# Gated recurrence and low-rank mixer on one core: a new instruction order, 96-row block totals, ReLU inside an add

## The chip, the cores and the metric

The kernel runs on one core of a Trainium2 chip. The metric is the device time of one execution in microseconds. Three executions of the kernel before took 645.2, 645.34 and 646.04 us; the median is 645.34. The profile is one further execution, 645.33 us, of which 643.6 us lie between its first and its last instruction (the span). TensorE's granted clock was 0.999 of full speed in it.

## The reference

There are two stages. The first is a gated linear recurrence with a complex gate, for 4 batches, 8 heads, 768 steps and a head width of 48:

```python
mag = np.sqrt(a_re * a_re + a_im * a_im)
scale = np.minimum(mag, 0.999) / (mag + 1e-06)
a_re_n, a_im_n = (a_re * scale, a_im * scale)
for t in range(S):
    new_re = ar * S_re - ai * S_im        # ar, ai: the gate at step t, per row of the state
    new_im = ar * S_im + ai * S_re
    kv = np.einsum('bhd,bhe->bhde', k[:, :, t], v[:, :, t])
    S_re, S_im = (new_re + kv, new_im)
    y[:, :, t] = np.einsum('bhd,bhde->bhe', q[:, :, t], S_re)
```

Its output, laid out as x with 4 batches, 768 tokens and 384 channels, goes through a mixer. It mixes tokens by a product of rank 32 and channels by two dense layers of width 1536:

```python
xt = x.transpose(0, 2, 1)
h = xt @ U @ V                            # U 768x32, V 32x768
u = x + h.transpose(0, 2, 1)
ch = np.maximum(u @ w_ch1, 0.0) @ w_ch2   # 384x1536, 1536x384
return (u + ch).astype(np.float32)
```

## The kernel before, in words

**Tiling.** The 3072 tokens (4 batches of 768) are cut into 24 chunks of 128. Two neighbouring chunks form a group, so there are 12 groups; six chunks (three groups) make a batch. A gate's decay is kept as a logarithm of its magnitude and a phase. Within a chunk the recurrence is written as products of scaled q, k and v; the state G is carried from chunk to chunk.

**Stages of a group.** `load_a` fetches a_re and a_im. `magnitudes` makes the log magnitudes `GL` with squares, logarithms and exponentials on ScalarE and adds on VectorE. For groups 3 to 11 (`SPLIT`) it also splits them into two parts for faster sums (`GS`). `within` makes running sums on TensorE and exponentials of them (`es`, `ef`). `totals` and `of_blocks` make sums of `GL` over 32 kinds of blocks of tokens, by products with the constant matrix `total` (line 711): for each chunk, four pairs of heads, the two heads of a pair in the lower and the upper half of the array's columns. ScalarE takes the exponential (`E`), and four transfers on SP's queue (line 697) place it in `T`, by which q and k are later scaled. `turns` and `angles` make the phases; a phase's last row is carried to the next chunk by a transfer on GpSimd's queue (line 750, `gate<-F`). `waves` makes cosines and sines (`cs`).

**Stages of a chunk.** `load_qkv` fetches q, k and v. `prep` scales and rotates q and k (`QKC`), and transposes them (`tr`, line 823) to `QK`. `chain` makes the products of neighbouring tokens (`inner`, lines 870 and 873; `corners`, line 937), picks them by masks into `DG`, places them by transfers into `AT` (line 924), scales `QK` by `T`, advances the state (`dk`, line 962, to `GM` and `G`), and makes the chunk's output `y` (lines 993 and 1001), which ScalarE copies to `xo`.

**Mixer.** `mixer(m)` takes two chunks, so there are 12 mixers, three a batch. The first of a batch needs all six chunks' `xo`: `rank` (line 1036) is their product with U, in 12 matrix products that accumulate in one tile, in four strips of 32 columns; ScalarE copies it to `r`. Then come the product with V (`mixed`, line 1052), an add to `xo`, the transposition `uTp` (line 1065), and the copy `uT` (line 1067), for each of its two chunks. `up` is the first dense layer (line 1077) with ReLU on ScalarE. From mixer 7 on (`FEWER`) `up_fewer` makes that layer from 15 products instead of 18 (`few`, line 1135): the first product to a part of `h` is copied there by ScalarE, later ones are added by VectorE, and a pass of ScalarE over `h` makes the ReLU. `down` and `down_two` (lines 1223 and 1266) are the second layer; their results are added to `xo` and stored.

**Weights.** A piece of w1, w2 or of U and V arrives as fp64 words (`stage`) and is converted by `single`: two scalings, a shift, an add, and a merge of the sign. Pieces with a number below `EARLY` have the scalings on VectorE, the others on ScalarE; the other three operations are VectorE's. The six pieces of w1 come first, then U and V, then the six of w2.

**What sets the order.** No scheduler orders the instructions when the kernel is built. Each operation is entered in a plan under an engine, a kind and a rank, and the table `ORDER` gives it its place; `Plan.order` sorts all operations by that number, and each engine runs its own in that order. SP and GpSimd issue their transfers in order too: a transfer that waits for a buffer holds back all that follow on the same queue. The table `SPARE` says how many filler products (`spare`, line 1396, whose result is not used) TensorE runs before an operation. There are 130 of them, all ahead of the first `up`. The costs in the calls (`PE(0.51, ...)`) are not used when the kernel is built.

## Time and profile before

| what | value |
|---|---|
| median of 3 runs | 645.34 us (645.2 to 646.04) |
| the profiled execution | 645.33 us |
| its span | 643.6 us |
| TensorE busy | 623.3 us (97%), 10242 records |
| weight loads busy | 552.9 us (86%) |
| VectorE busy | 515.3 us (80%), 933 instructions |
| ScalarE busy | 411.6 us (64%), 785 instructions |
| GpSimd busy | 38.4 us (6%) |
| transfers | 163316 packets, 45.72 MB; 153808 packets under 512 B |

Times are in microseconds from the span's start. A matrix product in fp32 appears as two records of TensorE, each with a weight load (PEld); a transposition and an fp32r product appear as one. "PE" in a busy share covers the filler too. `L379`, `L382` and `L376` are helpers (multiply, add, activation), so groups with these lines are told apart by their tiles. "SPq" is SP's queue: the time that it spent on issuing a transfer.

### The profile page before, as it was taken

To read this page: it belongs to the slowest core of one execution; us is meant where nothing else is said; L and a number is where in the kernel's file an instruction comes from. 1 tells how busy PE (TensorE), PEld (TensorE's weight loads), DVE (VectorE), ACT (ScalarE), POOL (GpSimd) and SP (SyncE) were. 2 spreads that over 40 slices of the span, in tenths; PEclk is the share of its full clock that TensorE was granted. 3 is DMA by queue.
4 is the path that set the end of the run, shared out by engine and by line. 5 is a ranking of instruction groups with operands and counts; after the bars stand their busy time and mean duration, and the time that the engine had idled before them with its cause. 6 is when DMAs were issued, how large, how long until landed. Compare 5 with 4: busy or idle time off the path is not lost.

```text
span 643.6 us, 23208 instructions
## 1 busy us (share of the span) xinstructions
PE 623.3 (97%) x10242; PEld 552.9 (86%) x10242; DVE 515.3 (80%) x933; ACT 411.6 (64%) x785; POOL 38.4 (6%) x79
## 2 busy tenths in 40 slices
PE   8998988999999999999999999999999999999997
PEld 7777777776889889789988988888999998999997
DVE  7999999687999879658969877787999884664653
ACT  7899988696887786666686786678355333212130
POOL 5000000000000000020020010010100000000010
PEclk9999999999999999999999999999999999999999
DMA  8755473625142362241331433411204010000010
GB/s 224 196 117 123 98 191 69 172 101 111 31 82 57 80 123 43 49 108 20 58 79 31 86 72 65 98 28 35 46 22 76 20 26 3 1 1 7 20 44 31
DMA packets 163316, 45.72 MB, mean 71 GB/s; under 512 B 153808, under 2 KB 160016, under 8 KB 163216
## 3 DMA queue, kind: packets, MB, share of 16 engines
q1 hardware_dynamic: 161008, 39.90, 28.6%
q0 software_dynamic: 2208, 4.35, 2.0%
q8 instruction: 80, 1.31, 0.9%
q14 instruction: 20, 0.16, 0.1%
HBM read 33.59 MB, written 4.72 MB: 60 GB/s over the span
## 4 chain that ended last, share of the span: by engine, by line
PE 76%; DVE 8%; DMA 5%; ACT 5%; SPq 3%; issue 2%; POOL 0%; DVEq 0%; ACTq 0%; POOLq 0%
PE down L1266 22%; PE up L1077 15%; PE few L1135 11%; PE tr L823 5%; PE y L1001 3%; PE dk L962 3%; PE inner L873 2%; PE y L993 2%; PE inner L870 2%; ACT gate L376 2%; DVE QK L379 1%; DMA qk<-in_k_dram 1%; PE mixed L1052 1%; PE mixed L1036 1%; DMA gate<-F 1%
## 5 line engine op out<-in xcount | busy, mean ns | idle before, releaser
L1077 PE MATMUL up<-uT,w 128*128 128x256 f32 x504 | 115.5, 381 | 1.3 <-ACT h L376 1.3
L379 DVE TENSOR_TENSOR QK<-QK,T 112x512 f32<-112x512 f32 (+2 forms) x144 | 102.6, 730 | 7.7 <-PE corners L937 3.3
L1077 PEld LDWEIGHTS up<-uT,w 128*128 128x128 f32 x504 | 93.5, 190 | 13.6 <-ACT h L376 1.7
L376 ACT ACTIVATE gate<-gate 128x768 f32<-128x768 f32 (+1 forms) x89 | 70.8, 799 | 11.5 <-DVE GS L759 5.6
L835 ACT COPY QK<-tr 112x512 f32<-112x512 f32 x96 | 53.7, 585 | 34.8 <-PE tr L823 34.3
L1266 PE MATMUL down<-w,h 128*128 128x192 f32 x396 | 73.1, 331 | 0.0
L1266 PEld LDWEIGHTS down<-w,h 128*128 128x128 f32 x396 | 64.0, 190 | 3.0 <-issue 2.0
L1143 ACT COPY h<-few 128x512 f32<-128x512 f32 x30 | 17.3, 586 | 66.6 <-PE few L1135 66.5
L823 PE MATMUL tr<-ident,QKC 128*112 128x128 f32 x384 | 53.9, 276 | 4.9 <-DVE QKC L379 3.4
L379 DVE TENSOR_TENSOR QKC<-qk,cs 128x768 f32<-128x768 f32 x48 | 45.5, 953 | 8.2 <-ACT cs L376 3.8
L823 PEld LDWEIGHTS tr<-ident,QKC 128*112 128x112 f32 x384 | 42.5, 133 | 11.1 <-DVE QKC L379 4.1
L382 DVE TENSOR_TENSOR h<-few,h 128x512 f32<-128x512 f32 x45 | 30.6, 689 | 22.2 <-PE few L1135 12.3
L382 DVE TENSOR_TENSOR xo<-down,xo 128x192 f32<-128x192 f32 (+1 forms) x79 | 30.1, 385 | 19.0 <-PE down L1266 18.9
L1396 PE MATMUL spare<-ident 128*128 128x128 f32 x260 | 40.1, 298 | 2.1 <-POOL ident masks.py:199 1.4
L1396 PEld LDWEIGHTS spare<-ident 128*128 128x128 f32 x260 | 35.5, 206 | 5.7 <-POOL ident masks.py:199 1.4
L1266 PE MATMUL down<-stage 128*128 128x192 f32 x198 | 37.4, 329 | 0.0
L1135 PE MATMUL few<-gate,w 128*128 128x128 f32 x280 | 36.4, 278 | 0.0
L1210 POOL DMA_DIRECT2D out_dram<-xo x32 | 18.8, 604 | 275.4 <-DVE xo L382 164.0
L1135 PEld LDWEIGHTS few<-gate,w 128*128 128x128 f32 x280 | 33.6, 192 | 0.4
L942 ACT COPY AT<-corners 32x128 f32<-32x128 f32 x96 | 24.3, 255 | 13.9 <-PE corners L937 12.4
L376 ACT ACTIVATE h<-up 128x512 f32<-128x512 f32 x42 | 24.6, 591 | 13.1 <-PE up L1077 13.1
L1266 PEld LDWEIGHTS down<-stage 128*128 128x128 f32 x198 | 32.1, 190 | 0.6 <-issue 0.2
(153 smaller groups left out, 1240.9 us busy)
## 6 DMA issues: line engine op xcount, KB each, us to landing
stage<-in_moe_w_ch_dram SPq DMA_DIRECT2D x12, 768.0 KB, 5.0
gate<-in_a_im_dram SPq DMA_DIRECT2D x24, 192.0 KB, 3.5
gate<-in_a_re_dram SPq DMA_DIRECT2D x24, 192.0 KB, 3.4
qk<-in_k_dram SPq DMA_DIRECT2D x24, 192.0 KB, 3.0
qk<-in_q_dram SPq DMA_DIRECT2D x24, 192.0 KB, 3.4
VP<-in_v_dram SPq DMA_DIRECT2D x24, 192.0 KB, 3.9
AT<-DG SPq DMA_DIRECT2D x96, 32.0 KB, 2.5
T<-E SPq DMA_DIRECT2D x48, 48.0 KB, 2.3
```

The lines of the kernel that those rows point to most:

```text
L376: return nc.scalar.activation(out=o, in_=i, func=f, **kw)
L379: nc.vector.tensor_tensor(out=o, in0=a, in1=b, op=OP.mult)
L382: nc.vector.tensor_tensor(out=o, in0=a, in1=b, op=OP.add)
L823: nc.tensor.transpose(out=get(*ps)[0:DQ, j], in_=get(*qkc)[:, hh * HH + j].rearrange("p u d -> p (u d)")[:, 0:DQ], identity=ident)
L835: nc.scalar.copy(out=to, in_=a)
L942: ACT(0.36, RR, lambda r=r, u=u: nc.scalar.copy(out=get(*ATi).rearrange("p (a u) t -> p a u t", u=2)[r:r + BLK, :, u, BLK:2 * BLK], in_=ge ...
L962: nc.tensor.matmul(out=get(*dk[r])[x:end, h], lhsT=get(*ks)[at, h, x // DP, 0:end - x], rhs=get(*VPi)[at, h], start=True, stop=True, tile_ ...
L1001: nc.tensor.matmul(out=get(*y[u])[side(r, u), p], lhsT=k_of(h, r * HC, HC), rhs=get(*(mid_G if r else ("G", i - 1)))[:, h], start=False, s ...
L1077: nc.tensor.matmul(out=get(*ps)[:, e], lhsT=w1[:, f, (ff + e) * 128:(ff + e + 1) * 128], rhs=get(*uT)[:, f], start=(f == 0), stop=(f == KD ...
L1135: nc.tensor.matmul(out=get(*ps)[:, q], lhsT=w()[:, q * 128:(q + 1) * 128], rhs=v[0](), start=(n == 0 and q == 0), stop=True, skip_group_ch ...
L1266: nc.tensor.matmul(out=get(*to)[:, part], lhsT=x(j), rhs=y[:, j], start=(first and j == 0), stop=(j == KH - 1), skip_group_check=not first)
L1396: nc.tensor.matmul(out=spare[0], lhsT=ident, rhs=ident, start=True, stop=True)
```

## The change

- Both tables, `ORDER` and `SPARE`, are replaced, so that operations of all engines stand in other places. The author's search for the new order allowed at most 3072 pieces of transfers under way at a time. There are 139 filler products.
- Block totals of groups 3 to 11: a pair of heads is one product with 96 columns of weights, four products a chunk in place of eight. `E` then holds the two heads of a pair in rows 0 to 47 and 48 to 95, and the four transfers to `T` write pieces of 32 elements in place of 128.
- `EARLY` is 4, and U and V are converted third, after two pieces of w1. So pieces 0, 1 (w1), 2 (U, V) and 3 (w1) are scaled on VectorE.
- Batch 0's `rank` is entered as three operations of four products, so that each can stand in a place of its own. The other batches' is one operation as before.
- The copy `uT` of a mixer's second chunk is ScalarE's; the first stays on VectorE.
- In `up_fewer`, the last add to a part of `h` is a custom VectorE operation that adds and limits the result to 0 and above; the pass for ReLU on ScalarE is dropped.

```diff
-    EARLY, SPREAD = 3, (0,)
+    EARLY, SPREAD = 4, (0,)
...
             for f in range(KD):
+                if p == 2:
+                    single(p, ("w1", p), ("UV", 0), UV, [tokens(moe_U), tokens(moe_V.rearrange("r (s m) -> (r s) m", m=m))])
+                    p += 1
+                    for n in range(NP):
+                        SP(0.45, ("load", 7), lambda n=n: nc.sync.dma_start(out=V[n * R:(n + 1) * R].rearrange("r (s m) -> r s m", m=m),
+                                                                   in_=UV[:, NCH * R:]), reads=[("UV", 0)], writes=[("V", 0, n)])
                 single(p, ("w1", p), ("w1", f, h), w1[:, f, h:h + WP], [tokens(moe_w_ch1[f * 128:(f + 1) * 128, h:h + WP])])
...
-                        in_=get(*e)[w * 64:w * 64 + D, 0:hi - lo].rearrange("p c h b -> p c (h b)")), [e], [tt + ((u, w),)])
+                        in_=get(*e)[w * 64:w * 64 + D, 0:hi - lo].rearrange("p c h b -> p c (h b)")) if g not in SPLIT else
+                       nc.sync.dma_start(out=get(*tt)[u * DP:u * DP + D].rearrange("p c (h w b) -> p c h w b", w=2, b=NTOT)[:, :, :, w],
+                                         in_=get(*e)[w * D:(w + 1) * D]), [e], [tt + ((u, w),)])
...
-            PE(0.51, R1, sums, [l, ("total", 0), ("sums", g)], [ps], way=1, takes=[e], steps=4 * HH)
+            def at_once():
+                for p in range(HH):
+                    h = (i - lo) * DM + p * 2 * D
+                    nc.tensor.matmul(out=get(*ps)[0:2 * D, p], lhsT=get(*l)[:, h:h + 2 * D], rhs=total, start=True, stop=True)
+            if g in SPLIT:
+                PE(0.4, R1, at_once, [l, ("total", 0), ("sums", g)], [ps], takes=[e], steps=2 * HH)
+            else:
+                PE(0.51, R1, sums, [l, ("total", 0), ("sums", g)], [ps], way=1, takes=[e], steps=4 * HH)
...
-            PE(2.07, R0, rank, [("UV", 0)] + [("xo", b * NCH + c) for c in range(NCH)], [ps], steps=2 * NP * NCH // MC)
+            rounds = range(NCH // MC)
+            for ks in [[k] for k in rounds] if b == 0 else [rounds]:
+                PE(0.69 * len(ks), R0, lambda ks=ks: rank(ks), [("UV", 0)] + [("xo", b * NCH + c) for c in range(NCH) if c % len(rounds) in ks] +
+                   [sums_r + (("k", ks[0] - 1),)] * (ks[0] > 0), [sums_r + (("k", k),) for k in ks], steps=2 * NP * len(ks))
...
-            DVE(c_dve(DM), R0, lambda: nc.vector.tensor_copy(out=get(*uT)[:, :, cc * CH:(cc + 1) * CH], in_=get(*tr)), [tr],
-                [uT + (cc,)])
+            to = lambda: get(*uT)[:, :, cc * CH:(cc + 1) * CH]
+            if cc:
+                ACT(c_act(DM) - 0.045, R0, lambda: nc.scalar.copy(out=to(), in_=get(*tr)), [tr], [uT + (cc,)])
+            else:
+                DVE(c_dve(DM), R0, lambda: nc.vector.tensor_copy(out=to(), in_=get(*tr)), [tr], [uT + (cc,)])
...
-                    else:
+                    elif left[to] > 1:
                         DVE(c_dve(n3 * CH), RU, lambda i=i, k=k: add(at(i, k), get(*ps), at(i, k)), [ps], [o])
+                    else:
+                        DVE(c_dve(n3 * CH), RU, lambda i=i, k=k: nc.vector._custom_dve(
+                            dve_ops.TENSOR_ADD_SAT, out=at(i, k), in0=get(*ps), in1=at(i, k), s0=math.inf, s1=0.0), [ps, o],
+                            [h + (n3 * i,), h + (n3 * i + 2,)])
-                    if not left[to]:
-                        ACT(c_act(n3 * CH) - 0.045, RU, lambda i=i, k=k: act(at(i, k), at(i, k), AF.Relu), [o],
-                            [h + (n3 * i,), h + (n3 * i + 2,)])
```

## The prediction

> **What bounds the kernel now.** I read the page's busy shares first, then busy time by stretch, then the waits of TensorE, and last the order of time where the first mixer begins.

> ```profile
> span 643.6 us, 23208 instructions
> ...
> PE 623.3 (97%) x10242; PEld 552.9 (86%) x10242; DVE 515.3 (80%) x933; ACT 411.6 (64%) x785; POOL 38.4 (6%) x79
> ...
> L1396 PE MATMUL spare<-ident 128*128 128x128 f32 x260 | 40.1, 298 | 2.1 <-POOL ident masks.py:199 1.4 <-issue 0.7
> ```
> ```profile
> 20.00:113.00 93.00, 83.25 (x2079) 67.58 (x2079) 88.79 (x148) 86.86 (x165) 0.00 (x0) 1.00 0.56 131
> ...
> 120.30:640.00 519.70, 515.93 (x7986) 465.88 (x7984) 404.09 (x736) 304.10 (x583) 29.79 (x47) 1.00 0.24 53
> ```
> ```profile
> PE up L1077 <- ACT h L376: 1.3, 1, 1.3
> PE y L1001 <- DVE QK L379: 1.1, 1, 1.1
> PE y L993 <- DMA AT<-DG: 0.7, 1, 0.7
> PE y L1001 <- issue: 0.4, 1, 0.4
> ```

> The columns of the stretches are length, then busy time of PE, its weight loads, VectorE, ScalarE, GpSimd. All of the 40 us of filler (`spare`) lies before the first mixer's `up`, so from 20 to 113 us a busy TensorE means little: VectorE is the bound (88.8 of 93 us, 4.2 idle). From 120.3 us, the first `up`, to 640 TensorE is busy 515.9 of 519.7 us, and its waits there (third fence) sum to 3.5. So there are two prices: what delays or hastens the first `up`, and what lengthens TensorE's own work after it. A shorter operation elsewhere pays only through one of these.

> **The change part by part.** All sums stand on the profiled execution (645.33, span 643.6; the median of the runs is 645.34, so nothing is converted).

> *Block totals (L711).* Eighteen blocks, two chunks for each of groups 3 to 11, go from eight 64- or 48-column products in two halves of the array to four 96-column ones. Two of them come before the first `up` beside filler; 16 lie in the saturated part.

> ```profile
> 180.62 0.65 PE L711 MATMUL tot<-total,GL 128*64 128x32 f32 x16
> 181.20 0.46 PE L937 MATMUL corners<-QK 112*32 112x32 f32 x32
> ```
> ```profile
> 474.23 1.06 PE L1135 MATMUL few<-gate 128*128 128x128 f32 x8
> 475.12 1.06 PE L1135 MATMUL few<-gate,w 128*128 128x128 f32 x8
> ```

> An fp32 product is two records. A block holds TensorE from 180.62 to 181.20, 0.58 us. By the trace's start times 0.09 of this is the change of the array's shape (the last `few` before an `inner` is followed after 205 ns, another `few` after 112), leaving 0.49. The loads of the 64-column half start 58 ns apart, those of the 48-column half 45, with only 32 columns streamed in either: weight loading sets the pace, and the halves load side by side. The new block is eight records in one row. If a 96-column load took no longer than the old pairs (0.49/8 = 61 ns), it would cost the same 0.49; if it took as long as a 128-column `few` (0.89/8 = 111), 0.89. By columns it lies between, 61 + 32/64 x 50 = 86, so 0.69: I take that, since 45, 58 and 111 rise evenly with the columns. That is +0.20 x 16 = +3.2 us. The instruction orders have 170 shape changes after the first `up` before and 166 after, -0.4. Sum +2.8, ends -0.4 (61 ns) and +6.0 (111). Fewer instructions, more time.

> [...]

> *Rank in three steps, end of the startup.*

> ```profile
> 110.84 0.56 DVE L382 TENSOR_TENSOR GM<-GM,dk 112x384 f32<-112x384 f32 x1 [0.43 <-PE dk L962]
> 112.65 0.64 PE L1001 MATMUL y<-G,QK 112*64 112x48 f32 x16
> 114.00 0.31 ACT L1012 COPY xo<-y 64x192 f32<-64x192 f32 x1
> 114.31 2.14 PE L1036 MATMUL mixed<-xo,UV 128*32 128x384 f32 x24
> 116.52 0.48 ACT L1039 COPY r<-mixed 128x384 f32<-128x384 f32 x1 [0.40 <-PE mixed L1036]
> 117.05 0.92 PE L1052 MATMUL mixed<-r,V 64*128 64x192 f32 x8
> 118.00 1.02 DVE L382 TENSOR_TENSOR xo<-mixed,xo 128x384 f32<-128x384 f32 x2 [0.21 <-PE mixed L1052]
> 120.34 7.98 PE L1077 MATMUL up<-uT,w 128*128 128x256 f32 x36
> ```

> Of batch 0's 24 records (114.31 to 116.38, 2.07 us) two thirds now run before the last chunk's `xo`, so `r` can be copied 1.38 earlier and V's product ends near 116.6. But VectorE then has its own queue: between its last `GM` add (111.3) and the `xo` add the new order holds 5.6 us of conversion, phase and cast work (by durations less their 0.08 overlap), so it arrives at 116.9, not 118.0. Gain 1.1; with the second `uT` copy on ScalarE beside the first, 0.1 more: -1.2. Ends: 0 (VectorE keeps a 1 us wait) and -1.5.

> *U, V third, third w1 piece (EARLY 4).* The first `up` needs them all in either order. Up to the first `xo` add VectorE's work by rows is 110.4 us before and 110.6 after; ScalarE's up to `r` 105.0 and 102.9. VectorE bounds, so I take 0; the ends are +0.2 and the 4.2 us that it idles. The V copies now stand on SP's queue ahead of loads of chunks 2 to 4 and wait for the conversion: what hides this is the time until those loads are used.

> *ReLU within the last add (L382 to a custom add), half of the uT copies to ScalarE.* Thirty ScalarE passes of 0.62 go (-18.7 us), 12 copies of about 0.47 come (+5.7); VectorE sheds 12 x 0.55, its add keeping its 0.69 (the custom form is as long as the plain one at 768 columns: 0.89 against 0.89). ScalarE is busy 304 of 519.7 us there and TensorE waits for `h` once, 1.3 us: priced at 0, ends 0 and -1.3. In that stretch ScalarE stands behind a phase that waits for a transfer (gate<-F); the new order still has one between the first two `h` copies.

> *T transfers (L697).* Nine groups' four go from 96 pieces of 512 B to 384 of 128 B. The `AT` row, 256 pieces of 128 B, lands in 2.5 us, T now in 2.3; so some 2.7. No instruction waits for T in the trace, and the last of these T transfers is issued 21 us or more ahead of the first read (350.4 against 372.0 us is the closest): 0, ends 0 and +0.4 x 9 = 3.6.

> *Filler* goes from 130 products to 139, all before the first `up`, where TensorE idles another 9.7 of 93 us: 0, ends 0 and +2.0 (9 x 0.22). *The end:* the last matmuls now feed a half-width add (0.36 for 0.56) and a 96 KB store (1.6 against 1.9): -0.5.

> Sum: 645.33 + 2.8 - 1.2 - 0.5 = **646.4**, no change to speak of (0.2%, 1.3 us, is about what a measurement tells from none). Own range, from the ends of the products and of the startup: 643 to 649.5.

> **The rivals.** *Transfers come free.* SP's issues are stalled now:

> ```profile
> 47.67 2.56 SPq L697
> 50.28 3.86 DMA gate<-in_a_im_dram
> ...
> 79.46 4.35 DMA qk<-in_k_dram
> ```

> An issue is 0.6 elsewhere. With fewer pieces under way VectorE could lose 3 of its 4.2 idle us and TensorE 1.5 of its 3.5: 641.9. For it: these pieces lie on the chain that ended last. Against: VectorE waits only 1.4 us for named loads between 20 and 113.

> *Loads come late (slower).* Holding loads back moves them towards their use: chunk 0's k is now 14th on SP's queue, behind two `a_re` loads that wait for the gate buffers, where both k loads stood in the first 12; chunk 4's q stands behind chunk 3's first DG copy. A late k costs VectorE 2.3 us at 396; two such in the startup make 4.6 us: 651. It decides once a load lands after VectorE has reached the chunk's weighing. Against: before the queue stalls, 2.2 and 2.9 us at 6 to 11 us, had the same effect.

> *Weight loads don't bind.* Eight records at the 31 ns that each of 16 takes now: 0.25 a block, -3.8 - 0.4 in place of +2.8: 639.4. Against: the 58 and 45 ns above. That a part is not carried out is excluded: the instruction order shows 96-column products, the steps of rank and the custom add.

> **Numbers.** Forecast 0.50 (of it 0.05 faster, 0.26 same, 0.19 slower), free transfers 0.20, late loads 0.20, unbound weight loads 0.10. So faster 0.35, same 0.26, slower 0.39. The range reaches from half-way into the two fast rivals to the slow one: 640.5 to 651.

> **What would show it.** A `tot` block of eight records spaced about 86 ns (60 or 110 would be wrong); the last third of `rank` 0.7 us before `r`, and the first `up` near 119.1; TensorE's waits after it near 3.5 us; no wait of `QK` for T. A first `up` before 116.5 or after 122, or TensorE waits over 7 us, would make the forecast wrong.

## The result, and the profile after

The changed kernel takes 649.53 us in the median of 20 executions (646.1 to 653.8), the kernel before 645.09 us in 20 executions beside them. The ratio is 1.0075, with a 95% interval from 1.0058 to 1.0091: 4.8 us slower (3.7 to 5.9). The forecast was 646.4 us. The range holds the result; the forecast's own range, up to 649.5, just misses it. A few executions of the experiments' kernels took 1000 us and more; no ratio below uses them.

The profiled execution took 651.5 us. The page of the changed kernel, first its span and busy shares, then the filler's group, then T's transfers (the last number is the median time from issue to landing):

```profile
span 649.7 us, 22911 instructions
...
PE 629.9 (97%) x10116; PEld 561.8 (86%) x10116; DVE 510.9 (79%) x923; ACT 398.2 (61%) x765; POOL 41.5 (6%) x79
...
L1413 PE MATMUL spare<-ident 128*128 128x128 f32 x278 | 44.5, 305 | 1.4 <-POOL ident masks.py:199 1.4
...
T<-E SPq DMA_DIRECT2D x48, 48.0 KB, 3.0
```

VectorE and ScalarE have less to do than before (4.4 and 13.4 us less), TensorE 6.6 us more on fewer records, GpSimd 3.1 us more on the same number of instructions. The next lines go by stretch, with the same columns as before (length, PE, weight loads, VectorE, ScalarE, GpSimd, granted clock, DMA share, GB/s). The kernel before in the first of these stretches, then the changed kernel in all four:

```profile
0.00:20.00 20.00, 16.78 (x120) 14.77 (x120) 15.21 (x38) 14.38 (x29) 8.65 (x32) 1.00 0.87 210
```
```profile
0.00:20.00 20.00, 15.31 (x103) 13.60 (x104) 13.36 (x34) 13.58 (x28) 11.78 (x32) 0.89 0.83 205
20.00:113.00 93.00, 84.33 (x1979) 70.14 (x1980) 87.50 (x150) 83.02 (x155) 0.00 (x0) 0.99 0.55 125
113.00:120.30 7.30, 5.65 (x142) 4.63 (x140) 5.94 (x8) 4.27 (x10) 0.00 (x0) 0.86 0.57 136
120.30:640.00 519.70, 517.94 (x7864) 466.98 (x7863) 400.77 (x725) 297.30 (x574) 29.67 (x47) 1.00 0.26 55
```

In each of the first three stretches VectorE and ScalarE get less done than before (from 113 to 120.3 us it was 6.67 and 6.27 us), and the granted clock, 1.00 in all of them before, is 0.89, 0.99 and 0.86. The first `up` starts at 126.85 us; it was 120.34. From there to the end it is 522.9 us, before 523.3. So all of the loss arises ahead of the first mixer, where the forecast had a gain of 1.2 us; and behind it two changes cancel. TensorE's waits behind the first `up`:

```profile
PE y L1003 <- DMA AT<-DG: 1.2, 2, 0.9
PE tr L833 <- ACT uT L1082: 0.2, 1, 0.2
```

They are 1.4 us where they were 3.5; the wait for `h` is gone. The block totals stand against that (one block in the timeline; the second number is the time of all eight records):

```profile
108.16 0.79 PE L719 MATMUL tot<-total,GL 128*96 128x32 f32 x8
```

By the start times in the trace these records are 85 ns apart. The 16 blocks behind the first `up`, each up to the start of what follows it, take 10.69 us, where the kernel before took 8.41.

VectorE's waits between 15 us and the first `up` (total, times, longest) show where the 6.5 us were lost:

```profile
DVE GS L768 <- ACT gate L375: 2.8, 1, 2.8
DVE gate L738 <- ACT gate L375: 2.4, 1, 2.4
DVE F L783 <- ACT F L375: 1.8, 2, 1.6
DVE QK L378 <- PE corners L947: 1.5, 2, 1.2
DVE QKC L378 <- PE dk L972: 1.5, 1, 1.5
```

Up to the first `up`, VectorE is busy 110.1 us (before 110.7) and idle 16.8 (before 9.6). The engines that it waits for wait themselves. Followed back through the timeline, three things come late in the order, and one more in this execution.

*`total`, at 15.8 us.* GpSimd makes the constant matrix `total` from `prefix` by sixteen small operations; the first `tot` needs it. The kernel before, then the changed kernel:

```profile
10.74 0.32 POOL L493 TENSOR_TENSOR total<-prefix 128x1 f32<-128x1 f32 x1
18.69 0.88 PE L767 MATMUL ph<-gate,prefix 128*128 128x384 f32 x2 [0.60 <-issue]
```
```profile
3.44 1.24 SPq L463 DMA_DIRECT2D prefix<-in_spans_dram  x1
6.60 0.40 POOL L468 TENSOR_TENSOR mid<-prefix 128x128 fp32r<-128x128 f32 x1 [3.32 <-DMA prefix<-in_spans_dram]
6.95 0.29 POOL L472 CAST prefix_r<-prefix 128x128 fp32r<-128x128 f32 x1
14.80 0.92 POOL L492 TENSOR_TENSOR total<-prefix 128x1 f32<-128x1 f32 x1
15.77 1.92 PE L713 MATMUL tot<-total,GL 128*64 128x32 f32 x32 [2.29 <-POOL total L492]
17.61 5.06 PE L1413 MATMUL spare<-ident 128*128 128x128 f32 x22
22.47 0.89 PE L777 MATMUL ph<-gate,prefix 128*128 128x384 f32 x2
```

`prefix` is issued fifth on SP's queue (before: fourth) and lands 1.0 us later, `prefix_r` now stands ahead of `total`, and the operations themselves are longer (7.4 us from the first to the last, before 4.5). `total` ends at 15.7 us (before: 11.0, with 3 us to spare until its use at 14.12), TensorE idles 2.3 us and its clock is then granted at half until 22.6 us, through `tot` and the filler behind it. The first phase product starts at 22.47 us; before, at 18.69.

*The picks of chunk 2 in `AT`, at 81 us.* VectorE writes the last pick into `DG` at 72.4 us:

```profile
72.44 0.29 DVE L895 COPY_PREDICATED DG<-mask,inner 128x128 f32<-128x128 int32 x1
72.94 0.99 SPq L516 DMA_DIRECT2D gate<-in_a_re_dram  x2
74.03 2.22 SPq L934 DMA_DIRECT2D AT<-DG  x2
76.37 0.54 SPq L525 DMA_DIRECT2D VP<-in_v_dram  x1
76.95 1.62 SPq L934 DMA_DIRECT2D AT<-DG  x2
81.33 0.92 PE L1003 MATMUL y<-VP,AT 64*64 64x48 f32 x32 [1.51 <-ACT gate L375]
```

The four transfers to `AT` stand on SP's queue behind two loads of a_re and around a load of v, so the last is issued 5.8 us after the pick. The bracket puts the wait of `y` down to ScalarE's `gate`; the operands of `y` are VP and AT, and an experiment below shows that it was AT.

*a_im, at 58 us.* ScalarE waits for the second load of a_im of a group, and `tr` and VectorE's next QK wait for ScalarE:

```profile
54.39 0.60 SPq L516 DMA_DIRECT2D gate<-in_a_im_dram  x1
58.20 0.84 ACT L375 ACTIVATE gate<-gate 128x768 f32<-128x768 f32 x1 [1.70 <-DMA gate<-in_a_im_dram]
60.40 0.65 PE L833 MATMUL tr<-ident,QKC 128*112 128x128 f32 x4 [1.56 <-ACT QK L845]
```

*The last transfer to `AT` of the startup, at 117.8 us.* The last chunk's `y` waits as well, and a second stretch at half clock, 118.2 to 121.6 us, follows:

```profile
110.98 3.18 SPq L934 DMA_DIRECT2D AT<-DG  x4
117.80 0.80 PE L1003 MATMUL y<-VP,AT 64*64 64x48 f32 x28 [1.65 <-ACT gate L375]
```

Here no load stands right ahead of the four transfers or between them. The last of them landed 4.2 us after it was issued, at 117.71 us by the trace. In the profiles of a1_keep_clock and c1_again (below) this took 2.0 us, and `y` did not wait.

Two theories follow. *A*: the clock costs the time. Over the 20 executions the mean granted clock and the time are correlated (-0.88); a line through them rises by 0.45 us for each us at half speed, and the median execution has some 10 us of it. *C* (the expectations' theory B comes to the same): the late transfers and the late `total` cost it, and the clock only follows TensorE's waits.

### The profile page after: what moved, and what is told of

It reads as the page before. It is cut to its first block, busy times and chain, and to the rows that moved or that the text cites. A ratio compares the mean times of both kernels' runs of the same rounds, so it can differ in the third digit from the quotient of the medians.

```text
span 649.7 us, 22911 instructions
## 1 busy us (share of the span) xinstructions
PE 629.9 (97%) x10116; PEld 561.8 (86%) x10116; DVE 510.9 (79%) x923; ACT 398.2 (61%) x765; POOL 41.5 (6%) x79
## 3 DMA queue, kind: packets, MB, share of 16 engines
q0 software_dynamic: 2208, 4.35, 2.0%
## 4 chain that ended last, share of the span: by engine, by line
PE 76%; ACT 6%; issue 6%; DVE 5%; DMA 3%; SPq 3%; POOL 2%; DVEq 0%; POOLq 0%; ACTq 0%
PE down L1283 22%; PE up L1093 13%; PE few L1151 10%; PE tr L833 5%; PE y L1011 3%; PE dk L972 3%; PE inner L883 3%; PE y L1003 2%; PE spare L1413 2%; ACT gate L375 2%; PE inner L880 2%; PE mixed L1065 1%; PE tot L719 1%; SPq L934 1%; DVE QK L378 1%
## 5 line engine op out<-in xcount | busy, mean ns | idle before, releaser
L1093 PEld LDWEIGHTS up<-uT,w 128*128 128x128 f32 x504 | 93.6, 190 | 11.7
L1413 PE MATMUL spare<-ident 128*128 128x128 f32 x278 | 44.5, 305 | 1.4 <-POOL ident masks.py:199 1.4
L1413 PEld LDWEIGHTS spare<-ident 128*128 128x128 f32 x278 | 39.2, 212 | 6.3 <-issue 2.0
L760 POOL DMA_DIRECT2D gate<-F x15 | 12.0, 799 | 406.9 <-DVE F L783 221.2
L972 PEld LDWEIGHTS dk<-VP,QKC 64*48 64x48 f32 (+1 forms) x1408 | 24.7, 127 | 7.8 <-issue 4.3
L1227 POOL DMA_DIRECT2D out_dram<-xo x32 | 19.2, 637 | 183.7 <-DVE xo L381 124.3
```

The source lines that it names most:

```text
L972: nc.tensor.matmul(out=get(*dk[r])[x:end, h], lhsT=get(*ks)[at, h, x // DP, 0:end - x], rhs=get(*VPi)[at, h], start=True, stop=True, tile_ ...
L1093: nc.tensor.matmul(out=get(*ps)[:, e], lhsT=w1[:, f, (ff + e) * 128:(ff + e + 1) * 128], rhs=get(*uT)[:, f], start=(f == 0), stop=(f == KD ...
L1413: nc.tensor.matmul(out=spare[0], lhsT=ident, rhs=ident, start=True, stop=True)
```

## The experiments

Each ratio is against executions of the kernel before beside it, with its 95% interval. The medians of those were 645.65 us in the first four runs, 645.58 in the next four and 644.81 in the last four.

### Does the clock cost the time?

**a1_keep_clock**: filler where TensorE idles.

```diff
-SPARE = {29: 23, 45: 2, 53: 1, 80: 11, ... 558: 2, 584: 1,
+SPARE = {29: 23, 45: 2, 53: 10, 80: 11, ... 558: 2, 565: 7, 584: 1,
```

> The changed kernel with 16 more filler products on TensorE: 9 ahead of the first block of `tot`, where it idles 2.3 us until 15.8 us, and 7 ahead of the last chunk's first `y` product, where it idles 1.6 us until 117.8 us. Nothing else is different. Theory A (the half-speed clock is the cost): the clock stays at full speed up to the first `up`, and the time falls by 0.45 us for each of the 10.4 us at half speed, the slope over the twenty runs: 645 to 646.5 us against 649.5, equal to the kernel before within 0.2%. Theory B (the waits themselves are the cost, the clock only follows them): the clock is full as well, but `total` and the picks in `AT` arrive as late as now, so the time stays at 648.5 to 649.5 us.

Measured: 649.68 us, ratio 1.0072 (1.0047 to 1.0097): nothing gained. In its profile the clock is full through the whole startup. But the sum is no clean test. `total` ended even later there (17.5 us), and yet the first `up` came at 123.49 us, 3.4 us sooner than in the changed kernel's profile. And at 262 us, behind a wait of 1.1 us, the clock fell for 13.6 us (windows from 6.6 us on, the first 256.0 us long):

```profile
6.60:262.60 256.00, 244.48 (x4477) 205.90 (x4477) 229.50 (x381) 212.95 (x397) 18.07 (x31) 1.00 0.49 110
262.60:276.20 13.60, 13.60 (x142) 10.92 (x146) 5.55 (x11) 7.97 (x18) 0.00 (x0) 0.50 0.13 25
```

This execution took 654.3 us, the slowest of its twelve, and 529.0 us of it from the first `up` to the end, 6.1 more than the changed kernel. So behind the first `up`, where TensorE is the bound, the fall cost nearly half of its length (an estimate from two executions). Three executions at 0.999 or more took 646.9 to 647.3 us, still above the kernel before.

Two runs on the kernel before test the clock by itself, once by adding a fall and once by removing one. **b1_gap** takes filler away:

```diff
-SPARE = {27: 20, 43: 3, 52: 1, 76: 12, 87: 3,
+SPARE = {27: 20, 43: 3, 52: 1, 87: 3,
```

> The kernel before, without the 12 filler products between the first `tot` and the first `ph`: TensorE idles 3.5 us from 15.2 us instead of running work whose result is not used. No wait of another engine is lengthened by that itself. Theory A (half speed is the cost): the clock falls to half for 3.4 or 6.8 us right behind the gap, the first phases come later, and the time rises by 1.5 to 4 us, to 646.5 to 649 us. Theory B (the clock only follows the waits and costs next to nothing): the clock falls and the time stays at 645.1 us within 0.5.

Measured: 645.96 us, ratio 1.0000 (0.9983 to 1.0016). The fall is there, right behind the gap:

```profile
15.00:18.60 3.60, 0.21 (x1) 0.24 (x2) 3.57 (x8) 2.48 (x5) 0.00 (x0) 1.00 0.85 165
18.60:22.10 3.50, 3.50 (x11) 2.35 (x11) 3.01 (x6) 2.33 (x5) 0.00 (x0) 0.51 0.95 203
```

TensorE spends 3.4 us at half speed there and the time doesn't move. **b4_fill** adds filler:

```diff
-        ... 406: 2, 423: 5, 426: 1, ...
+        ... 406: 2, 423: 12, 426: 1, ...
```

> The kernel before with 7 more filler products ahead of the `tr` at 87 us, where TensorE idles 2.1 us; in most runs of the kernel before the clock was at half speed for 3 to 6.5 us, and the traces of two of its variants show that fall at 80 and 87 us. If the half-speed clock is a cause (the slope over the 32 runs of the kernel before, 0.34 us for each us at half speed): the clock is full in most runs and the time is 643.5 to 644.3 us, faster than before by 0.2 to 0.3%. If the clock only follows waits that cost the time themselves (b1_gap: a second fall cost nothing): 645.2 to 646 us, no change.

Measured: 645.26 us, ratio 1.0005 (0.9985 to 1.0025). The mean clock was 0.999 or more in 10 of 12 executions, against 14 of 35 of the kernel before beside it. So the filler does what it is for, and the time stays. By the mean granted clocks b1_gap added 2.2 us of half speed and b4_fill took 2.8 us away; at 0.45 us each that would have been 1.0 and 1.3 us. The intervals leave 0.15% or so, 1 us: under VectorE's work in the kernel before, the slope of 0.45 isn't a price.

For the new order no run settles it, and the traces speak for a price there. Between VectorE's fifth and sixth add of `dk` to the state, the changed kernel and then a2_total_early (below) have the same work, and `y` waits for AT 1.51 and 1.52 us. In the second 6.8 us at half speed follow this wait, in the first none:

```profile
79.38:90.54 11.16, 9.21 (x191) 7.22 (x191) 9.79 (x17) 9.56 (x17) 0.00 (x0) 1.00 0.65 125
```
```profile
76.46:90.25 13.79, 12.10 (x191) 9.65 (x191) 9.79 (x17) 9.55 (x17) 0.00 (x0) 0.75 0.59 118
```

In a3_old_totals, with 3.4 us at half speed, the stretch takes 12.6 us, and in the five other profiles of the new order, all without a fall in it, 10.5 to 11.8. So part of the correlation may be a price. With one exception, the fall in a1_keep_clock at 262 us, every fall that these traces show in full follows a stretch in which TensorE idled for 1.4 us or more, 2.29 and 1.62 us in the changed kernel's (see the last section). So waits stand ahead of the clock in either theory.

### Do the late arrivals cost it?

**a2_total_early**: `prefix` and `prefix_r` in the places of the kernel before.

```diff
-    ("SP", "load"): {0.1: [5], ...
+    ("SP", "load"): {0.1: [3.5], ...
-    ("POOL", "load"): {0: [25], 1.5: [26], 2: [27], 1: [28]},
+    ("POOL", "load"): {0: [25], 1.5: [28.5], 2: [27], 1: [28]},
```

> The changed kernel with the load of `prefix` fourth on SP's queue in place of fifth, and GpSimd's copy `prefix_r` after `total` in place of ahead of it, both as in the kernel before. `total` should be ready some 1.2 us sooner, by 14.5 us in place of 15.7, and TensorE's idle time before the first `tot` is 1.1 us in place of 2.3, so that the first fall of the clock goes; the second, at 118 us, stays possible. Theory A (half speed is the cost): 646 to 647.5 us, above the kernel that only adds filler. Theory B (lateness is the cost): at least as good as that one, with the first chunks 1.3 us earlier than there, and 645.5 to 647 us where the filler alone gives 648.5 or more.

Measured: 648.26 us, ratio 1.0033 (1.0010 to 1.0055), some 2.7 us better than the changed kernel, and less than either theory expected. `total` ends at 11.2 us, the first phase product starts at 19.2; the first `up` starts at 123.38. The waits for a_im and for chunk 2's picks are still there, at 55 and 78 us; the last chunk's `y` doesn't wait, though the loads stand where they stood.

**c3_queue**: three places of SP's queue.

```diff
...
-    7: [249, 177, 515, 400, 257, 217, 211, 253, 256]     # V, a_re, a_im
+    7: [257.5, 177, 515, 400, 257, 217, 211, 250.5, 252.5]
-    6: [251]                                             # v
+    6: [256.5]
-    8: [373], 9: [454, 326, 325, 420, 379]               # v, a_re: behind chunk 2's picks
+    8: [375.2], 9: [454, 375.4, 375.3, 420, 379]
-    11: [544, 543, 581, 612, 580]                        # a_re: away from the last chunk's picks
+    11: [573.4, 573.3, 581, 612, 580]
...
```

> The changed kernel with the three edits to SP's queue of c1_startup alone; `prefix`, `prefix_r` and `total` stay as they are. Theory C, with the three places about additive: 1.3 us (what a2_total_early gained) above c1_startup, at 646 to 648 us; the first `tot` still waits for `total` until 15 to 17 us, the later waits are gone. Theory A': 649 to 650 us.

Measured: 648.60 us, ratio 1.0059 (1.0031 to 1.0086): about 1 us, less than was expected, and with this interval not told from nothing by itself. In its profile the waits for a_im and for chunk 2's picks are gone, but the last chunk's `y` still waits, although the loads of a_re now stand further back:

```profile
108.43 3.52 SPq L934 DMA_DIRECT2D AT<-DG  x4
115.40 0.67 PE L1003 MATMUL y<-VP,AT 64*64 64x48 f32 x28 [1.80 <-ACT gate L375]
```

The last of the four took 4.0 us to land. So moving the loads didn't remove this wait; the last section says what the trace shows ahead of it.

**c1_startup** makes the edits of both.

> The changed kernel with `prefix` and `total` early (as in a2_total_early) and SP's queue put in another order at three places of the startup: chunk 2's four picks to `AT` go ahead of the two loads of a_re and the load of v that stand before and between them; the second load of a_im, for which ScalarE waits 1.7 us at 56.5 us, goes 3 us up; the two loads of a_re right behind the last chunk's picks go behind the next load of a weight. Theory C (the new order loses its time in the startup to transfers and to `total` that come late, TensorE's clock adding little): the waits of `y` for `AT` at 79 and 116 us (1.5 and 1.7 us) and of `gate` for a_im go, the first `up` comes at 119.5 to 121 us against 123.4 in a2_total_early and 126.8 in the changed kernel, and the time is 644.5 to 646.5 us. Theory A' (what is lost beside the products is mainly the clock): no better than a2_total_early, 647.5 to 649 us.

Measured: 646.37 us, ratio 1.0011 (0.9997 to 1.0025). The same kernel ran again, for another profile, as **c1_again**:

> c1_startup once more, for a profile of it that is undisturbed. Theory C: TensorE waits for `AT` and ScalarE for a_im no longer at 56, 79 and 116 us, VectorE idles some 3 us less before the first `up` than in a2_total_early (13.0 us), the first `up` comes at 119.5 to 121 us, and the time is 645.5 to 647.5 us again, within 0.3% of the kernel before.

Measured: 646.80 us, ratio 1.0034 (1.0013 to 1.0056). The first run is on the forecast of theory C, the second within its time but not within its 0.3%; the two together say 0.1 to 0.3% above the kernel before, in place of 0.75%. The profile (span 644.3 us) shows the three places of the order mended:

```profile
10.11 0.52 POOL L492 TENSOR_TENSOR total<-prefix 128x1 f32<-128x1 f32 x1
14.36 1.09 PE L713 MATMUL tot<-total,GL 128*64 128x32 f32 x32 [0.19 <-ACT es L375]
15.38 2.72 PE L1413 MATMUL spare<-ident 128*128 128x128 f32 x22
19.12 0.88 PE L777 MATMUL ph<-gate,prefix 128*128 128x384 f32 x2 [1.03 <-ACT gate L375]
...
69.34 3.15 SPq L934 DMA_DIRECT2D AT<-DG  x4
76.32 1.13 PE L1003 MATMUL y<-VP,AT 64*64 64x48 f32 x32
```

The same 22 records of filler take 2.72 us at full clock where they took 5.06, `y` starts without a wait, and the wait that the bracket had put down to `gate` went when the transfers to AT were moved: it had been theirs. ScalarE's wait for a_im is gone, too. The milestones of the startup, and what follows it (us, one execution each):

| kernel | last chunk's `GM` add | first `up` | from there to the end |
|---|---|---|---|
| before | 110.84 | 120.34 | 523.3 |
| changed | 115.18 | 126.85 | 522.9 |
| a2_total_early | 114.82 | 123.38 | 523.0 |
| c3_queue | 112.62 | 124.46 | 522.2 |
| c1_again | 111.28 | 119.85 | 524.4 |

The first `up` of c1_again came 7.0 us sooner than the changed kernel's, the end 5.4: 1.6 us went back to waits behind it, in part to the wait for `h`, which is there again with 1.3 us. That fits a head start that a late first `up` gives the engines that feed TensorE: in the other profiles of the new order, a1_keep_clock apart, the last column is 522.2 to 523.0 where the first `up` comes after 123 us and 523.7 to 524.6 where it comes before 122.

The table and the times don't divide the loss alike. By the times the early `total` gains 2.7 us and the queue about 1, and c1_again, at 1.0034, is level with a2_total_early at 1.0033. By the table the early `total` alone brings the last `GM` add only 0.4 us forward and the queue 2.6. The rest of a2_total_early's 3.5 us at the first `up` is the wait at 117.8 us with the fall behind it, which it doesn't have: from the add to the first `up` it is 11.7 us in the changed kernel, 11.8 in c3_queue and 8.6 in the other two. The two edits together mend most of the loss; what each is worth is not shown by one profile each.

### What do the block totals cost?

**b2_96** makes this part alone in the kernel before (the two hunks `at_once` and the transfers of line 697, as in the change).

> The kernel before with one part of the change alone: the block totals of groups 3 to 11 as four products of 96 columns a chunk, with the transfers to T in pieces of 32 elements; the order is kept. By the records (85 ns each in place of 58 and 45 for a pair that loads side by side) 16 blocks after the first `up` cost 2.3 us more: 647.5 to 648.5 us against 645.6. If the price is covered by waits that shrink in turn: 645 to 646.5 us. If T's transfers in small pieces come late as well: over 649 us, with waits of `QK` for T.

Measured: 648.56 us, ratio 1.0047 (1.0029 to 1.0066): +3.0 us (1.9 to 4.3), the upper end of the first expectation. The records behind the first `up` took 11.5 us against 8.4, and TensorE waited nowhere for T.

**a3_old_totals** and **c2_startup_old** undo it, in the changed kernel and in c1_startup.

```diff
-            if g in SPLIT:
+            if False:
                 PE(0.4, R1, at_once, ...
-            used = 2 * D if g in SPLIT else 64 + D
+            used = 64 + D
```

> The changed kernel with the block totals of groups 3 to 11 as before: eight products of 64 and 48 columns a chunk and transfers to T in pieces of 128 elements; all places in the order are kept. Theory A: the 128 records of 96 columns after the first `up` took 10.69 us against 8.41 for the 256 records of the kernel before, so this part costs 2.3 us and the time falls to 647 us (646.5 to 648); the startup and its clock stay as they are. Rival (weight loads of a block lie under other work, or the shape changes that come back cost as much): 649 to 650 us.

> The same as c1_startup, with the block totals of groups 3 to 11 as in the kernel before (eight products a chunk, transfers to T in pieces of 128 elements). If the products of 96 columns cost what their records say, 10.7 against 8.4 to 9.1 us after the first `up`, this is 1.5 to 2.3 us below c1_startup: 642.5 to 645 us, the fastest of all and at or below the kernel before. If their price is covered (a3_old_totals gained nothing that could be told), the two are the same within 0.7 us.

Measured: a3_old_totals 649.49 us, ratio 1.0054 (1.0033 to 1.0076); c2_startup_old 647.83 us, ratio 1.0030 (1.0013 to 1.0048). The first is 0.2% below the changed kernel, with intervals that allow no gain as well as the whole 3 us. The second is a little above c1_startup beside it, so it doesn't gain what b2_96 lost. The records did become shorter (9.08 us for 10.69 in both), but the wait of `y` for AT behind the first `up` became longer, by 0.6 and 1.0 us; TensorE's waits of c2_startup_old there, then those of c1_again:

```profile
PE y L1003 <- DMA AT<-DG: 1.4, 2, 0.8
PE up L1093 <- ACT h L375: 1.4, 2, 1.0
```
```profile
PE up L1093 <- ACT h L375: 1.3, 2, 1.0
PE y L1003 <- DMA AT<-DG: 0.4, 2, 0.2
```

So the price of a product seems to depend on the order it stands in: 3 us where TensorE had work ready behind it, little where the next thing on TensorE waits for a transfer. The price of 3 us is shown; that the wait takes it back rests on one profile each.

### What do the steps of `rank` gain?

**d3_rank_one**: c1_startup with batch 0's `rank` as one operation.

```diff
-            for ks in [[k] for k in rounds] if b == 0 else [rounds]:
+            for ks in [rounds]:
-    ("PE", "small"): {0: [560, 583, 584, 586, 588, 590],
+    ("PE", "small"): {0: [584, 586, 588, 590],
```

> c1_startup with batch 0's `rank` as one operation of twelve products again, behind the last chunk's `xo`. The prediction's term: the steps gain 1.1 us in front of the first `up`, so this one is 1.1 us slower than c1_startup (1.4 by the records that then stand between `xo` and `r`), at 647.5 us. Rival (VectorE's queue is what the first `xo` add waits for): the same as c1_startup within 0.4 us.

Measured: 647.48 us, ratio 1.0044 (1.0025 to 1.0062), 0.7 us above c1_again beside it: between the two expectations, and the intervals allow both. The traces say less than the forecast: from the last `GM` add to the first `up` it is 8.82 us here, 8.57 in c1_again and 9.50 in the kernel before. One piece already starts with the chunks that are ready: its first record runs at 115.42 us, ahead of the last two copies to `xo` (115.45 and 115.78). In the kernel before eight records of filler stand in front of it.

**b6_rank_fill** takes the steps into the kernel before (`rank` itself as in the change), with b4_fill's filler:

```diff
-    ("PE", "small"): {0: [582, 584, 586, 588],        # rank, mixed, two uTp
+    ("PE", "small"): {0: [576.3, 576.6, 576.9, 584, 586, 588],
-    ("ACT", "small"): {0: [583, ...                   # r
+    ("ACT", "small"): {0: [577.5, ...
-    ("DVE", "w2"): {... 2: [580, 596, 604],
+    ("DVE", "w2"): {... 2: [590.5, 596, 604],
-        ... 564: 2, 582: 4, 584: 2, ...               # filler ahead of rank
+        ... 564: 2, 584: 2, ...
```

> b4_fill with batch 0's `rank` as three operations: two thirds can run ahead of the last copy of the last chunk's `xo`, `r` is copied ahead of a conversion on ScalarE, and VectorE's conversion of 0.56 us ahead of the `xo` add goes behind the `uT` copies. `r` comes some 1 us sooner and the `xo` add, for VectorE's own queue, 0.5 us sooner: 0.5 us below b4_fill. If the first `up` is bound by VectorE's earlier work alone: equal to b4_fill within 0.3 us.

Measured: 646.85 us, ratio 1.0025 (1.0003 to 1.0047). That misses both expectations. The stretch did become shorter, 9.13 us against 9.50 (in b4_fill 9.50), and the kernel 1.6 us slower than b4_fill. Its profile has `r` 1.1 us sooner, but the product with V starts 0.8 us after `r` is there, and there are more waits behind the first `up` (1.8 us for `h`, 0.9 ahead of `tot`, 0.7 for QK). Which moved operation causes them was not tried and stays open.

None of the twelve runs is faster than the kernel before.

## Why the prediction was right or wrong

**Block totals, +2.8: right, in the order it was worked out for.** The spacing is 85 ns (86 was taken from the column counts), and the part alone costs 3.0 us (1.9 to 4.3). By the records it is 2.3 us in the changed kernel. What the prediction had not said is that the time need not follow the records: c2_startup_old gained nothing by the old products.

**"The first `up` needs them all in either order ... VectorE bounds, so I take 0; the ends are +0.2 and the 4.2 us that it idles": this step failed.** VectorE's busy time was forecast well (110.7 us before, 110.1 after), but the step took VectorE's idle time as something that could only shrink. It grew by 7.2 us. The order of SP's queue and of GpSimd was read for what is used first by VectorE; `total`, AT and a_im reach VectorE through TensorE and ScalarE. In the kernel before, no product of the startup waited for `total` or AT, and a_im cost ScalarE 0.7 us. The view of waits can't show such a price ahead: `total` was ready 3 us before its use and had no line there. Of the 6.5 us at the first `up` 4.3 are there at the last `GM` add; the other 2.2 are the wait at 117.8 us and the fall behind it, which the places in the order don't explain.

**The slow rival, 651 us with 0.20, had the mechanism and about the size** (649.53 in the median), but the wrong places. The range holds the result only because it reaches to this rival, which is luck as far as the places go. No line of VectorE's waits names chunk 0's k or chunk 4's q. Its condition, a load that lands after VectorE has come to need it, was too narrow: what landed late was needed by the other engines. With the startup mended the kernel is 0.1 to 0.3% above the one before, and the forecast's terms gave 1.1 us, 0.17%: they describe c1_startup in their sum, and the 2.6 to 4.1 us between it and the changed kernel are the missed step. Term by term they agree less: c1_again's first `up` came 0.5 us sooner than before (forecast 1.2), and the rest took 1.2 us longer (forecast 2.3).

**The rank steps, -1.2: the size was off.** From the last `GM` add to the first `up` c1_again is 0.9 us shorter than the kernel before, of which 0.25 is left when `rank` is one piece against three; the rest is the order around it. In the changed kernel itself the stretch was 2.2 us longer, by the wait for AT at 117.8 us and the fall behind it. The sign posted for it ("a first `up` ... after 122 ... would make the forecast wrong") came true with 126.85.

**The tail, -0.5: right.** From the start of TensorE's last record to the end it was 3.81 us and is 3.34.

**ReLU in the add and the copies `uT`, 0: right as far as the waits show;** no run makes these parts alone. TensorE's wait for `h` is 1.3 us before and in c1_again, and gone only where the first `up` is late. **T's smaller pieces, 0: right**; they land in 3.0 us (estimated 2.7) and nothing waits for them. **Filler, 0:** the 11 products between `tot` and `ph` took 5.06 us at half clock in one execution, and the first phase came behind them; that such a stretch costs time was not found in b1_gap.

**Free transfers and free weight loads** are out: SP's issues are as long as before in the places above (3.2 us for four), and records 85 ns apart are not 31.

The clock was not in the prediction at all. It is what catches the eye first in the result. In the kernel before, adding or removing a fall moved nothing; what falls cost in the new order stays open. They follow waits: of the executions of c1_startup and c1_again, where waits are mended, 10 of 22 have a mean clock of 0.999 or more, of the changed kernel's none of 20.

## What to carry to other kernels

When an order is rewritten, compare for each transfer and each constant how long it was ready ahead of its use, not only who waits now: an arrival with 3 us of slack has no line in the waits, and it is the one that a new order can make late. On a queue that issues in order, put what the next product needs ahead of prefetches, and test a suspected wait by moving the transfer, since the name behind a wait may be that of an engine that came last by chance, and a wait that stays when the transfer is moved has another cause. A clock that falls in step with the time isn't yet its cause: take the fall away with filler, or add one, before pricing it.

## What the runs showed of the hardware that was not expected

*A longer fall.* In a1_keep_clock the clock went to half for 13.6 us after 256.0 us at full speed. TensorE was busy throughout the fall (13.60 of 13.60 us), and in the window ahead of it it idled 1.1 us, less than ahead of any other fall. It was seen in one profile only, and what sets it off was not found.

*A load of instructions in front of a transfer.* In the changed kernel and in c3_queue the last transfer to AT took 4.2 and 4.0 us to land, in a1_keep_clock, c1_again and d3_rank_one 2.0. In the two slow traces a packet of 16 KB on the queue for instructions (from 115.53 to 116.49 us, and from 113.31 to 114.26) ends as the transfer's last sixteen pieces start, 1.3 us behind all the others. In c1_again such a packet starts at 111.47 us, when the last piece is already under way. So it seems a matter of timing whether such a load stands in the way; that it held the sixteen pieces back is read from their times and was not tested.

*GpSimd's small operations take longer beside a busy VectorE.* The operations that make `total` on one column of 128 rows took 0.18 us beside an idle VectorE (at 7.74 us in the kernel before, at 7.54 in c1_again) and the time of VectorE's instruction beside a busy one, as in the changed kernel (spans of GpSimd are rough, but here they pair off):

```profile
13.38 0.94 DVE L381 CUSTOM_DVE_ANT_0 w<-w,stage 128x1536 uint16<-128x1536 uint16 x1
13.46 0.91 POOL L492 TENSOR_TENSOR total<-prefix 128x1 f32<-128x1 f32 x1
14.25 0.54 DVE L557 TENSOR_SCALAR stage<-stage 128x768 int32<-128x768 uint32 x1
14.31 0.52 POOL L491 COPY total<-prefix 128x1 f32<-128x1 f32 x1
```

From its first operation to its last `total` took 7.4 us in the changed kernel, 4.5 before and 4.0 in c1_again, where it runs earlier; VectorE idled 0.1, 0.9 and 1.3 us of that time. What ties the two engines is not shown. That a change which packs VectorE more tightly lengthens what GpSimd does beside it is an estimate from these three profiles.
